# Linformer attention and a SwiGLU block on one core: VectorE's and GpSimd's side work at other tiles, half of the diagonal k' copies on ScalarE

## The chip, the cores and the metric

The kernel runs on one core of a Trainium2 chip. The metric is device microseconds of one execution; of a set of runs the median is given.

## The reference

Attention over 8 batches, 8 heads, 1024 tokens and head dimension 64, in which `E` and `F` first project the 1024 keys and values to 64 each, and then a SwiGLU block over the 8192 tokens with 512 model and 1536 inner dimensions. Inputs and output are float32.

```python
k_proj = np.einsum('ks,bhsd->bhkd', E, k)
v_proj = np.einsum('ks,bhsd->bhkd', F, v)
scores = 1.0 / np.sqrt(64) * np.matmul(q, k_proj.transpose(0, 1, 3, 2))
attn = softmax(scores)                      # the row maximum is subtracted first
x = np.matmul(attn, v_proj)                 # heads side by side: (8192, 512)
g = x @ w_gate
out = (g / (1 + exp(-g)) * (x @ w_val)) @ w_out
```

## The kernel before

**Tiles and slots.** The 8192 tokens are 16 chunks `c` of 512, two for each batch. The SwiGLU of a chunk takes 12 tiles `f`, one for each 128 of the 1536 inner columns; a loop written out by hand runs over all 192 tiles `t`. Each tile has two slots, 2t and 2t+1. In a tile come, in this order: the gate matmul (`f_g`, L536), what is put at slot 2t, the value matmul (`f_v`), the list `late[t]`, what is put at slot 2t+1. The order in which this Python issues work is the order of every engine's queue. `place(b)` puts the attention of batch b into the 24 tiles from slot s0 = 48(b-1) on. Those 24 tiles are called the turn of batch b below, and tiles and slots are counted from its start: tiles 0 to 11 are chunk 2b-2, tiles 12 to 23 are chunk 2b-1. Tiles 0 to 23 of the turn of batch 2 are tiles 24 to 47 of the whole.

**SwiGLU of a tile.** ScalarE takes silu of the gate from PSUM (`th`, L563; in some tiles as tanh with two VectorE steps, L560, L681, L684, since tanh needs no change of ScalarE's table beside exp), and VectorE multiplies it with the value product into `hT` (L678). From chunk 3 on the value products of pairs of tiles are made in seven smaller products instead of eight (`p_34`, `p_1`, `p_52`, `p_76`, matmuls at L616). They need sums of x (`p_x`, L607: m = 4, 3, 1 and 6 with 7 together) and sums of the weights (`p_w`, L595). Their results are put together by a ScalarE copy (L644), VectorE sums (L647, L627) and the product with silu (L634, which needs both tiles' silu, L646 and L556). L652 is ScalarE's copy of product 1.

**Down projection.** The 1536x512 product for chunk c-1 is made during chunk c, likewise in seven products m for each of two halves p (`f_m`, matmuls at L762, in the order m = 3, 4, 5, 2, 1, 6, 7). They need sums of `hT` (`h_sum`, L745): m = 5 and 2 by GpSimd in 12 small pieces a chunk, m = 1, 6 and 7 by VectorE in one piece each. After m = 4 ScalarE copies (L779) and GpSimd adds (L781); after m = 6 VectorE adds the m = 1 product out of PSUM (L791) and GpSimd subtracts (L792, after L791); the m = 7 product adds to the region that L791 reads, so it waits for L791; after it VectorE writes the output tile (L797, which needs L792), and SP sends it. For p = 0 the products 1 and 6 lie in tile 4 of the chunk and 7 in tile 5, for p = 1 in tiles 10 and 11.

**Attention of a batch.** `u_KV` projects k and v; ScalarE and VectorE copy the results (L195, L200). `u_KT` turns k' and writes it in four copies into the diagonal tile `BD` (L298, L299), from which the score matmuls read (`u_S`, L378). There are eight parts of the scores, each with an exponential on ScalarE into one of four buffers `ee` (L386), a row sum and reciprocal on VectorE (`u_R`, L408, L409), and the normalised product on GpSimd (`u_N`, L423, called N below, with a small running sum `zsum`, L439). Part 7 uses the buffer of part 3. SP turns q (`u_TD`, L355) and the probabilities (`u_AD`, L362) by DMA; `u_PVt` multiplies with v' (L482), and ScalarE copies to `xT` (L491). A ScalarE change between exp and silu is a table load. The loads of the next batch's k, v and q go through GpSimd's queue.

**The watch.** `u_sum` and `u_flag` add `zsum` up and make a flag out of it with a one-column matmul (L902, L903, L907); all engines read the flag near the end, and only if it is set does a second, general program run.

Of the kernel before, what the change touches and what calls it, by code (L numbers as in the profile page):

```python
# [26 lines left out]
NFT = DFF // P  # L27
# [4 lines left out]
HF = NFT // 2  # L32
# [11 lines left out]
def kernel(  # L44
# [19 lines left out]
    nc = tc.nc  # L64
# [98 lines left out]
    def bank(where, shape, dt, name):  # L163
        if where == "a" and ring["wide"]:
            where = "aaz"[ring["n"] % 3]
            ring["n"] += 1
        if where == "v":
            v_turn[0] ^= 1
        pool, tag = banks[where]
        if where in "vw":  # L170
            tag += str(v_turn[0] ^ (where == "w"))
        return pool.tile(shape, dt, name=name, tag=tag)

    def copy(eng, out, in_):
        (nc.scalar.copy if eng is nc.scalar else eng.tensor_copy)(out=out, in_=in_)
# [94 lines left out]
    def turn_ksp(t, b, g):  # L270
        nc.tensor.matmul(
            out=t[:, 2 * g : 2 * g + 2, :].rearrange("p a k -> p (a k)"),
            lhsT=ksp[b][:, 2 * g : 2 * g + 2, :].rearrange("p h d -> p (h d)"),
            rhs=ident_bf[:],
            start=True,
            stop=True,
        )

    def u_KT(b, at="a", prs=(0, NPAIR)):

        t = bank(at, [P, NPAIR, KP], FP32, "kTp")
        for pr in range(*prs) if b > 1 or maxed else ():
            nc.tensor.matmul(
                out=t[:, pr, :],
                lhsT=ks[b % 2][:, 2 * pr : 2 * pr + 2, :].rearrange("p h d -> p (h d)"),
                rhs=ident_bf[:, 0:KP],
                start=True,  # L290
                stop=True,
            )
        for g in range(2) if b < 2 and not maxed else ():
            turn_ksp(t, b, g)
        bd = BD[b % 2][:].rearrange("p (a c) k -> p a c k", c=2)
        for c in range(2):
            src = t[64 * c : 64 * c + 64, slice(*prs)]
            nc.vector.tensor_copy(out=bd[0:64, slice(*prs), c, 0:64], in_=src)  # L298
            nc.vector.tensor_copy(out=bd[64:128, slice(*prs), c, 64:128], in_=src)  # L299

    def u_KT0(prs, ats, engs):
# [558 lines left out]
    def put(s, fn, *a):  # L860
        slots[s].append((fn, a))

    def place(b):
        s0 = 48 * (b - 1)
        if b == 1:
            put(22, u_TD, 1, 0)
            put(29, u_K1, 1)
            put(32, u_KT, 1)
            put(40, u_V1, 1)
            sa = (35, 36, 37, 38, 41, 42, 43, 44)  # L870
            put(41, u_AD, 1, 0)
            put(30, u_TD, 1, 1)
            put(47, u_AD, 1, 1)
            put(46, u_PVt, 1, 0, (0, 1), ("aa", "av"))
        else:
            if b == 2:
                put(s0 + 10, u_KV, b)
            else:
                put(s0 + 8, u_KV, b, "kv", (0, H), "v")
            put(s0 + (13 if b == 2 else 11), u_KT, b)  # L880
            put(s0 + (9 if b == 2 else -6), u_TD, b, 0)
            put(s0 + (11 if b == 2 else -4), u_TD, b, 1)
            sa = [s0 + j for j in ((15, 15, 17, 17) if b == 2 else (13, 13, 15, 15)) + (25, 25, 27, 27)]
            put(s0 + 29, u_AD, b, 0)
            put(s0 + 42, u_AD, b, 1)
            put(s0 + 44, u_PVt, b, 0, (0, 1), ("aa", "yz"))
        for j in range(NJ):
            put(sa[j], u_S, b, j)
            at = sa[j] + 1 if b == 1 else s0 + (
                16, 17 + (b > 2), 20, 22, 31, 33, 36, 38)[j]  # L890
            put(at, u_R, b, j)
            put(at, u_N, b, j)
        put(s0 + (68 if b == 1 else 56), u_PVt, b, 1, (0, 1), ("aa", "yz"))
# [20 lines left out]
    def general():  # L914
# [6 lines left out]
        with tc.For_i(0, B) as turn, tc.manual_schedule():  # L921
            turn_of.append(turn)
            b = 0
            load_k(b)
            load_v(b)
            u_KV(b)
            u_KT(b)
            for ch in range(CH):
                c = CH * b + ch
                load_q(b, ch)  # L930
                for u in range(4 * ch, 4 * ch + 4):
                    u_T(b, u)
                    u_S(b, u)
                    u_R(b, u)
                    u_N(b, u)
                    u_A(b, u)
                u_PVt(b, ch, (0, 1), ("aa", "yz"))
                for f in range(NFT):
                    f_g(c, f)
                    f_v(c, f)  # L940
                for m in (1, 2, 5, 6, 7):
                    h_sum(c, m, 0, HF, nc.vector)
                for n in range(14):
                    f_m(c, n)

    with tc.manual_schedule():
# [3 lines left out]
        for i in range(2):  # L950
            nc.scalar.dma_start(
                out=kraw[i][:],
                in_=k[0, 2 * i : 2 * i + 2].rearrange("h (p j) d -> p h (j d)", j=NJ),
# [125 lines left out]
        for b in range(1, B):  # L1079
            place(b)  # L1080
        for b in range(2, B):
            s0 = 48 * (b - 1) - (20 if b == 3 else 24)
# [10 lines left out]
        late = defaultdict(list)  # L1093
# [4 lines left out]
        for c in range(1, NC):  # L1098
            for f in range(HF):
                for m in (5, 2):  # L1100
                    at = (8, 7, 11, 11, 10, 11)[f] if c > 2 else HF + f
                    late[c * NFT + at].append((h_sum, c, m, f, f + 1))
            if c == NC - 1:
                late[c * NFT + HF + 1].append((h_sum, c, 6, 0, HF, nc.vector))
                for f in (0, 2, 4):
                    for m in (1, 7):
                        late[c * NFT + HF + f + 1].append((h_sum, c, m, f, f + 2, nc.vector))
            else:
                for i, m in enumerate((1, 6, 7)):
                    late[(c + 1) * NFT + 1 + i].append((h_sum, c, m, 0, HF, nc.vector))  # L1110
                for n, f in enumerate((0, 1, 2, 3, 4, 4, 5, 6, 7, 8, 9, 10, 10, 11)):
                    late[(c + 1) * NFT + f].append((f_m, c, n))

        for p, ts in ((5, (26, 27, 28, 28, 28)), (8, (29, 29, 31, 31, 31)), (2, (42, 42, 43, 43, 43))):
            for m, t in zip((1, 2, 5, 6, 7), ts):
                late[t].append((p_w, m, p))
        for c in range(3, NC):
            for i, m in enumerate((4, 3, 1, 67)):
                if c == 3:
                    t = c * NFT + (2, 2, 3, 3)[i]  # L1120
                elif c % 2:
                    t = c * NFT - (7, 7, 3, 3)[i]
                else:
                    t = c * NFT + (-1, -1, 0, 0)[i]
                late[t].append((p_x, c, m))
        for p, cs in PAIRED.items():
            for c in cs:
                late[c * NFT + p].append((p_1, c, p))

        for s, fn in ((38, u_sum), (40, u_flag), (88, u_bad)):  # L1130
            put(48 * (B - 2) + s, fn)
        for t in range(NIT):
            c, f = divmod(t, NFT)
            ring["wide"] = c < 2
            i = 1 if t < 2 else None
# [42 lines left out]
```

## Time and profile before

| | |
|---|---|
| median of 3 runs | 564.73 us (564.32 to 565.6) |
| the profiled execution | 566.03 us |
| its span, first to last instruction | 564.5 us |
| mean granted TensorE clock | 0.997 |
| busy: PE, VectorE, GpSimd, ScalarE | 532.3, 429.3, 324.2, 289.6 us |

The profile is one execution. Its page gives busy times and the chain of work that ended last; further views give, for every engine, who waited for whom, and the instructions in order of time. In timeline rows the columns are start in us, duration in us, engine, line, operation, tiles, shapes and count; brackets hold the idle time of the engine before the instruction and what ended it. The ends of matmuls are modelled.

### The profile page before, as it was taken

How to read it: one execution, taken by the hardware profiler on the slowest of the kernel's cores; microseconds unless marked ns; L12 is line 12 of the kernel's file. 1: busy time of each engine (PE TensorE's matmuls, PEld its weight loads, DVE VectorE, ACT ScalarE, POOL GpSimd, SP SyncE). 2: the span in 40 equal slices, each digit the busy share in tenths (PEclk: the TensorE clock that was granted, in tenths of full speed). 3: DMA queues.
4: the chain of work that ended last, by engine and by line, in shares of the span. 5: the costliest groups of instructions: out<-in, count | busy, mean ns of one | idle time of the engine just before them, and what ended most of it. 6: DMA issues, size and time to landing. Idle time of an engine off the chain costs nothing.

```text
span 564.5 us, 9975 instructions
## 1 busy us (share of the span) xinstructions
PE 532.3 (94%) x3712; PEld 336.1 (60%) x3780; DVE 429.3 (76%) x724; ACT 289.6 (51%) x515; POOL 324.2 (57%) x428
## 2 busy tenths in 40 slices
PE   7999999998999999999999999999999997999996
PEld 4654445565566566566666566666666655566665
DVE  3787886759878788787887787877977878586664
ACT  3564363763456634646546464564455662453431
POOL 6861593555824967068661786437773465534344
PEclk9999999999999999999999999999999999899999
DMA  9999979749800598007961199213990121200113
GB/s 198 191 198 189 186 130 177 143 97 199 190 2 37 105 212 169 38 1 152 198 135 39 39 162 222 66 39 75 164 244 4 39 74 39 74 6 35 38 39 114
DMA packets 112228, 62.94 MB, mean 112 GB/s; under 512 B 65968, under 2 KB 103856, under 8 KB 112176
## 3 DMA queue, kind: packets, MB, share of 16 engines
q0 software_dynamic: 43952, 29.49, 36.5%
q1 hardware_dynamic: 67392, 31.46, 22.4%
q10 hardware_dynamic: 832, 1.31, 0.8%
q8 instruction: 30, 0.49, 0.4%
q14 instruction: 22, 0.18, 0.1%
HBM read 60.29 MB, written 16.78 MB: 137 GB/s over the span
## 4 chain that ended last, share of the span: by engine, by line
PE 74%; DVE 15%; issue 5%; POOL 3%; DMA 2%; ACT 2%; DVEq 0%; ACTq 0%; POOLq 0%
PE gps L536 22%; PE yps L762 19%; PE vps L536 16%; PE vps L616 8%; DMA wv<-in_moe_w_val_dram 2%; PE kvp L187 2%; PE sc L378 2%; DVE hs L745 2%; PE yps L696 2%; DVE sx L627 2%; DVE ts L647 1%; PE pv L482 1%; DVE hT L678 1%; DVE hT L634 1%; DVE zr L408 1%
## 5 line engine op out<-in xcount | busy, mean ns | idle before, releaser
L536 PE MATMUL gps<-xT,wg 128*128 128x512 bf16 (+1 forms) x727 | 193.0, 378 | 1.8
L745 POOL TENSOR_TENSOR hs<-hT 128x256 bf16<-128x256 bf16 x180 | 125.8, 729 | 5.7 <-DVE hT L678 4.9
L536 PE MATMUL vps<-xT,wv 128*128 128x512 bf16 (+1 forms) x459 | 118.9, 376 | 1.4 <-DMA wv<-in_moe_w_val_dram 0.8
L762 PEld LDWEIGHTS <-hs 128*128 128x128 bf16 x900 | 88.1, 98 | 34.0 <-issue 13.5
L536 PEld LDWEIGHTS <-wg 128*128 128x128 bf16 x776 | 74.3, 98 | 52.0 <-issue 1.1
L423 POOL TENSOR_TENSOR AAd<-ee,zr 128x512 bf16<-128x512 f32 x56 | 62.5, 1115 | 64.9 <-DVE zr L409 34.9
L563 ACT ACTIVATE th<-gps 128x512 f32<-128x512 f32 x82 | 49.0, 597 | 95.2 <-PE gps L536 86.9
L792 POOL TENSOR_TENSOR tt<-tt,ysb 128x512 f32<-128x512 f32 x28 | 35.6, 1273 | 95.9 <-DVE tt L791 95.9
L762 PE MATMUL yps<-ws,hs 128*128 128x256 bf16 x540 | 68.6, 272 | 10.6 <-DVE tt L791 10.5
L536 PEld LDWEIGHTS <-wv 128*128 128x128 bf16 x480 | 45.2, 98 | 50.9 <-issue 6.5
L678 DVE TENSOR_TENSOR hT<-th,vps 128x512 bf16<-128x512 f32 x82 | 55.4, 676 | 26.1 <-PE vps L536 22.0
L634 DVE TENSOR_TENSOR hT<-thp,sx 128x512 bf16<-128x512 f32 x74 | 56.8, 767 | 6.8 <-ACT thp L556 2.2
L781 POOL TENSOR_TENSOR tt<-xs 128x256 f32<-128x256 f32 x30 | 29.9, 997 | 55.1 <-ACT xs L779 55.1
L627 DVE TENSOR_TENSOR sx<-ts,vps 128x512 f32<-128x512 f32 x74 | 50.1, 677 | 15.0 <-PE vps L616 12.8
L762 PE MATMUL yps<-ws,hT 128*128 128x256 bf16 x360 | 48.8, 273 | 0.5
L762 PE MATMUL yps<-wo,hs 128*128 128x256 bf16 x360 | 49.0, 274 | 0.1
L745 DVE TENSOR_TENSOR hs<-hT 128x1536 bf16<-128x1536 bf16 (+1 forms) x49 | 48.2, 989 | 0.0
L644 ACT COPY sx<-vps 128x512 f32<-128x512 f32 x37 | 21.7, 586 | 51.4 <-PE vps L616 50.8
L408 DVE TENSOR_REDUCE zr<-ee 128x8 f32<-128x512 f32 x64 | 43.2, 674 | 4.9 <-ACT ee L386 4.9
L762 PEld LDWEIGHTS <-hT 128*128 128x128 bf16 x360 | 35.2, 98 | 13.2
L681 DVE SCALAR_TENSOR_TENSOR s<-th,gps 128x512 f32<-128x512 f32 x35 | 23.6, 673 | 21.6 <-ACT th L560 20.8
L647 DVE TENSOR_TENSOR ts<-sx 128x256 f32<-128x256 f32 x37 | 27.0, 729 | 16.7 <-ACT sx L644 16.2
(135 smaller groups left out, 741.6 us busy)
## 6 DMA issues: line engine op xcount, KB each, us to landing
out_dram<-ysb SPq DMA_DIRECT2D x27, 512.0 KB, 2.9
qb<-in_q_dram POOLq DMA_DIRECT2D x14, 512.0 KB, 16.9
kb<-in_k_dram POOLq DMA_DIRECT2D x7, 1024.0 KB, 8.9
vb<-in_v_dram POOLq DMA_DIRECT2D x7, 1024.0 KB, 13.9
wo<-in_moe_w_out_dram POOLq DMA_DIRECT2D x2, 768.0 KB, 21.6
out_dram<-ysb SPq DMA_DIRECT2D x6, 256.0 KB, 2.4
kraw<-in_k_dram ACTq DMA_DIRECT2D x2, 512.0 KB, 4.9
qb<-in_q_dram POOLq DMA_DIRECT2D x4, 256.0 KB, 8.0
```

Of the source, the lines that this page charges most:

```text
L408: nc.vector.reduce_sum(out=z, in_=e[:], axis=AX.X)
L423: eng.tensor_tensor(out=a.rearrange("p j h k -> p h j k"), in0=ee.pop((b, u))[:], in1=r.unsqueeze(3).to_broadcast([P, 4, 2, KP]), op=ALU.mult,
L536: nc.tensor.matmul(out=ps[:, ts], lhsT=(wg, wv)[w][:, kt, f * P : (f + 1) * P], rhs=x[:, kt, ts], start=(kt == 0), stop=(kt == NKT - 1),)
L563: nc.scalar.activation(out=th[:], in_=ps[:], func=AF.Silu)
L616: nc.tensor.matmul(out=ps, lhsT=w[:, kt], rhs=xs[:, kt], start=(start and kt == 0), stop=(kt == 1), skip_group_check=True,)
L627: nc.vector.tensor_tensor(out=out, in0=a.unsqueeze(1).to_broadcast([P, 2, HT]), in1=b, op=op)
L634: nc.vector.tensor_tensor(out=h, in0=th, in1=v, op=ALU.mult)
L647: nc.vector.tensor_tensor(out=ts[:, 0], in0=sx[:, 0], in1=sx[:, 1], op=ALU.add)
L678: nc.vector.tensor_tensor(out=hT[c][:, f, :], in0=th[:], in1=ps[:], op=ALU.mult)
L745: eng.tensor_tensor(out=hs[c, m][:, fs, :], in0=quarter(hT[c], *a)[:, fs], in1=quarter(hT[c], *b)[:, fs], op=op,)
L762: nc.tensor.matmul(out=ps, lhsT=lhsT, rhs=ws[m][:, f, :] if rhs is None else rhs, start=(start and f == 0), stop=(f == HF - 1), skip_group ...
L792: nc.gpsimd.tensor_tensor(out=t[:], in0=t[:], in1=yo[c, p][:, 1:3], op=ALU.subtract)
```

## The change

Five things move, and one changes engine. In `u_KT`, for batches from 2 on, the two copies into rows 0 to 63 of `BD` go to ScalarE. In `place`, the row sums and products of all eight parts go to later slots, and the second turn of the probabilities from slot 42 to 43, which is behind the first turn of the next batch's q on SP's queue. The VectorE sum for m = 7 goes from tile 3 of a chunk to tile 4, behind L791. The weight sums for p = 2 go from tiles 42 and 43 to 32 to 35, and one for p = 8 from tile 31 to 30. The sums of x for the odd chunks go from 7 and 3 tiles before the chunk (2 and 3 tiles into it for chunk 3) to its first tile; for even chunks they stay. The watch's sum and flag go from slots 38 and 40 of the last batch to 44 and 50.

```diff
@@ u_KT @@
         for c in range(2):
             src = t[64 * c : 64 * c + 64, slice(*prs)]
-            nc.vector.tensor_copy(out=bd[0:64, slice(*prs), c, 0:64], in_=src)
+            copy(nc.scalar if b > 1 else nc.vector, bd[0:64, slice(*prs), c, 0:64], src)
             nc.vector.tensor_copy(out=bd[64:128, slice(*prs), c, 64:128], in_=src)
@@ place @@
-            put(s0 + 42, u_AD, b, 1)
+            put(s0 + 43, u_AD, b, 1)
...
             at = sa[j] + 1 if b == 1 else s0 + (
-                16, 17 + (b > 2), 20, 22, 31, 33, 36, 38)[j]
+                17, 17 + 2 * (b == 2), 21 if b == 2 else 19, 23, 35, 37, 40, 41)[j]
             put(at, u_R, b, j)
             put(at, u_N, b, j)
@@ the list late @@
-                for i, m in enumerate((1, 6, 7)):
+                for i, m in enumerate((1, 6)):
                     late[(c + 1) * NFT + 1 + i].append((h_sum, c, m, 0, HF, nc.vector))
                 for n, f in enumerate((0, 1, 2, 3, 4, 4, 5, 6, 7, 8, 9, 10, 10, 11)):
+                    if n == 6:
+                        late[(c + 1) * NFT + 4].append((h_sum, c, 7, 0, HF, nc.vector))
                     late[(c + 1) * NFT + f].append((f_m, c, n))
...
-        for p, ts in ((5, (26, 27, 28, 28, 28)), (8, (29, 29, 31, 31, 31)), (2, (42, 42, 43, 43, 43))):
+        for p, ts in ((5, (26, 27, 28, 28, 28)), (8, (29, 29, 30, 31, 31)), (2, (32, 33, 33, 34, 35))):
...
             for i, m in enumerate((4, 3, 1, 67)):
-                if c == 3:
-                    t = c * NFT + (2, 2, 3, 3)[i]
-                elif c % 2:
-                    t = c * NFT - (7, 7, 3, 3)[i]
-                else:
-                    t = c * NFT + (-1, -1, 0, 0)[i]
+                t = c * NFT + (0 if c % 2 else (-1, -1, 0, 0)[i])
                 late[t].append((p_x, c, m))
...
-        for s, fn in ((38, u_sum), (40, u_flag), (88, u_bad)):
+        for s, fn in ((44, u_sum), (50, u_flag), (88, u_bad)):
             put(48 * (B - 2) + s, fn)
```

## Prediction

> **What bounds the kernel now.** The page first: which engine is busy and what the last chain is made of.
>
> ```profile
> PE 532.3 (94%) x3712; PEld 336.1 (60%) x3780; DVE 429.3 (76%) x724; ACT 289.6 (51%) x515; POOL 324.2 (57%) x428
> PE 74%; DVE 15%; issue 5%; POOL 3%; DMA 2%; ACT 2%; DVEq 0%; ACTq 0%; POOLq 0%
> ```
>
> PE sets the time; a gain must come out of its 32 us that are not busy. So next the waits of PE alone (waiter, releaser: total us, times, longest).
>
> ```profile
> PE yps L762 <- DVE tt L791: 10.5, 11, 1.0
> PE sc L378 <- DVE BD L299: 4.5, 10, 0.7
> PE vps L616 <- DVE sx L627: 2.4, 2, 2.1
> PE bad L907 <- DVE sane L903: 2.2, 1, 2.2
> ```
>
> All four are VectorE being late in its queue. The timeline shows behind what. The steady turn is 67.26 us (the wait at 237.54 in the chain returns at 304.80), and each of batches 3 to 7 holds three such stalls; I read the turn of batch 4.
>
> ```profile
> 235.89 0.41 DVE L607 TENSOR_TENSOR xsa<-xT 128x512 bf16<-128x512 bf16 x1
> 236.23 0.41 DVE L298 CAST BD<-kTp 64x256 bf16<-64x256 f32 x1
> 237.54 0.43 DVE L299 CAST BD<-kTp 64x256 bf16<-64x256 f32 x1
> 238.02 0.55 PE L378 MATMUL sc<-BD,qTd 128*128 128x128 bf16 x7 [0.68 <-DVE BD L299]
> ...
> 250.34 0.68 DVE L408 TENSOR_REDUCE zr<-ee 128x8 f32<-128x512 f32 x1
> 251.73 0.41 DVE L791 TENSOR_TENSOR tt<-tt,yps 128x256 f32<-128x256 f32 x1
> 252.20 0.81 PE L762 MATMUL yps<-ws,hs 128*128 128x256 bf16 x6 [1.04 <-DVE tt L791]
> 255.05 1.04 POOL L423 TENSOR_TENSOR AAd<-ee,zr 128x512 bf16<-128x512 f32 x1
> 256.23 3.80 POOL L745 TENSOR_TENSOR hs<-hT 128x256 bf16<-128x256 bf16 x6
> 258.91 1.13 ACT L386 ACTIVATE ee<-sc 128x512 f32<-128x512 f32 x2
> 263.99 0.95 DVE L745 TENSOR_TENSOR hs<-hT 128x1536 bf16<-128x1536 bf16 x1
> 264.86 0.68 DVE L408 TENSOR_REDUCE zr<-ee 128x8 f32<-128x512 f32 x1
> 268.03 0.41 DVE L791 TENSOR_TENSOR tt<-tt,yps 128x256 f32<-128x256 f32 x1
> ```
>
> (1) Tile 5: two x sums and four k' copies stand before the first scores. (2) Tile 10: a row sum stands before L791, for which the seventh product waits. (3) Tile 16: the m=7 sum and a row sum stand before L791. A gap counts from the modelled end of the matmul before, about 0.17 us late (six matmuls of 0.11 from 236.09 end at 236.75; the score matmul starts at 237.12 with a gap of 0.21). So the stalls cost PE 0.38 + 0.85 = 1.23, 1.20 and 1.09 us: 3.5 a turn, 17.6 over five turns. Before them, in chunk 3, PE loses 0.79, 2.24, 0.37 and 0.46 us (131 to 145 us), 3.9 in all. The flag's matmul loses 2.34 at 479.18, and more follows it, in the windows by stretch (PE, PEld, DVE, ACT, POOL, then granted clock, DMA share, GB/s):
>
> ```profile
> 479.00:481.00 2.00, 1.82 (x14) 1.46 (x15) 1.23 (x4) 1.05 (x2) 1.59 (x3) 0.77 0.75 171
> 481.00:484.00 3.00, 3.00 (x14) 1.61 (x13) 0.59 (x2) 1.00 (x3) 1.54 (x3) 0.59 0.27 61
> ```
>
> Right after that gap TensorE runs below full clock: (1-0.77)x2 + (1-0.59)x3 = 1.7 us lost. No other stretch of the steady part does so, not even after the 2.24 at 137.16.
>
> **The change, part by part.** No arithmetic is added. Twelve copies (L298, 0.42 us each, 5.0 us) leave VectorE and come to ScalarE. ScalarE's price for 64x256 is not shown; its copies of 64x128 take 0.26 and of 64x512 0.59, its 128x256 0.37, so I take 0.37 (0.26 to 0.59): 0.74 a turn.
>
> *Tile 5.* The x sums (0.33 + 0.33 of queue) and two copies (0.85) go from before the scores. In their place: the m=7 sum (0.95) now follows L791 of tile 4, and the m=7 product waits for it. L791 starts at 232.77, the sum runs 233.15 to 234.10, PE was ready at 233.79: a new stall of 0.36. GpSimd's L792 (1.27), which would start at 233.33, waits for the sum and ends at 235.3; L647 waits for L792 (ends 235.6), L797 follows to 236.2, the two copies end at 236.55 and 236.98. ScalarE's two copies run after L652, 235.70 to 236.45, so they are not last. PE is ready at 236.75 + 0.36 = 237.11 and runs through. The second score matmul starts at 237.15 instead of 238.02: 0.9 gained net. Exp's table load now waits for the scores; the exponentials end at 239.9 instead of 239.46, but th(7) is done at 240.5, when L681 can start on VectorE anyway (240.4): nothing.
>
> *Tile 10.* Row sums 0 and 1 now both stand behind L647 of tile 8, 0.83 each, row sum 2 before the second L627, and two x sums (1.88 at 247.21) are gone. From L647 at 243.0: L647 0.45, two row sums 1.65, L627 0.66, L634 0.8, row sum 0.85, L627 0.7, L634 1.3 (held by an N product, as the L634 of 1.02 at 137.21 was), L678 0.65, L791 0.4: 250.45. PE is ready at 251.00 - 0.9 = 250.1 to 250.2. So 0.25 is left of 1.20: gained so far 1.75.
>
> *Tiles 11 to 17.* Here the change pays back. Row sum 3 moves from slot 22 to 23, behind L797, and its product N (L423) on GpSimd behind eight h sums instead of two. The eight run from 251.8 (L792's end): 8 x 0.645 = 5.2. At the same time the four x sums now stand at tile 12, two x sums more than there is quiet room for: those beside GpSimd's sums take 0.89 where they take 0.42 alone, and each holds GpSimd for about 0.4. I take 1.6 for the four (0.9, what the eight sums at 284.56 to 290.64 took over 5.2, to 2.0). So N runs from 258.45 to 259.5, where it ended at 256.09. The exponential of part 7 writes the buffer which that N reads, so it starts at 259.55: it was 259.46. ScalarE has then given back all that PE had won: L644, table load, L646, L652, L556 end at 263.6 (263.26). L634 goes 263.6 to 264.25, then L627, L634, L678, L791 end at 266.65, the m=7 sum at 267.5. The product starts at 267.55; it was 268.49. Kept: 0.9 a turn. Each us that N is earlier or later moves this by one, with a ceiling of about 1.9 from L791 and the sum in a row; bounds -0.1 to 1.9.
>
> [...]
>
> *Tiles 17 to 23.* Row sums 4 to 7 go to slots 35, 37, 40, 41. Each is 0.83 before an L627, and PE's next use of that bank is ready 0.1 or more after; nothing taken, 0.3 a turn if that cover is gone. The second transpose of the probabilities (slot 43) now stands on SP behind the q transpose, which waits for q to land (issued at 263.22, 16.2 us): its own landing moves from 285.8 to about 289. PV takes it at 295.17 - 0.9, so 5 us cover it; beyond, each us is a us.
>
> *Chunk 3 (tiles 36 to 47).* Stall 2.24 is L647 held from 131.93 to 135.12 by a q load, L792 and an N in a row; now q goes ahead and N behind. Of 0.79 some 0.25 stays for the m=7 sum; of the last two some 0.4. Gained 3.2 (2.0 to 3.8). The five weight sums for p=2 (0.28 clear, at worst 1.4 each) go to tiles 32 to 35, where VectorE idles 0.5 to 1.8 us a tile: nothing.
>
> *The flag.* Its sum stands at tile 22, where the last N has ended at about 280.4 on the turn's scale, as the sum comes up; the matmul comes three tiles later: 2.3 gained (1.8 to 2.34), and the 1.7 of slow clock.
>
> [...]
>
> **Sum.** 5 x 0.9 + 3.2 + 2.3 + 1.7 = 11.7 from the profiled execution, 566.03 us (span 564.5 and 1.5 around it): 554.3. The median of the runs, 564.73, is 1.3 lower, about the slow clock, which I assume it did not have: 564.73 - 10.0 = 554.7. I say 554.5.
>
> **Rivals.** *VectorE and GpSimd share better*: N ends a us earlier, 1.9 a turn; 554.5 - 5.0 = 549.5. For it: GpSimd idles 2.85 us before its N at 251.40, and the new order fills that. *The gain is given back whole*: N a us later, 0 a turn; only chunk 3 and flag count, 564.7 - 5.5 = 559 to 559.7. For it: the walk leaves 0.1 us at tiles 8 to 10, where VectorE is never idle. *Slower*: N, behind h sums and x sums, holds the exponential of part 7. From 2.0 us later than I have it (261.5) a turn loses 1.1, and five turns eat the 5.5 of flag and chunk 3; at 2.7 later a turn loses 1.8: 564.7 - 5.5 + 9 = 568. Against it: that needs the x sums to cost GpSimd over 3.6. That the change does not do what it says is excluded by the order of its instructions.
>
> **How the numbers follow.** Forecast 0.5; better sharing 0.25; given back 0.16; slower 0.08; 0.01 for the rest. Range: -0.1 to 1.9 a turn with chunk 3 and flag from 3.8 to 6.1 gives 549.1 to 561.4; with the spread of the runs (564.32 to 565.6) I say 548.5 to 561.5. A measurement here tells 0.2%, 1.1 us, from no change: faster 0.90, same 0.03, slower 0.07.
>
> **What would show it.** Right: PE's waits for BD gone, those for L791 replaced by shorter ones for L745 before L762, none on L907, no clock below 1 near 480; N of tile 11 ends after its eight h sums, and L386 waits for POOL. Wrong: a turn over 67.3 or under 65 us, or PV L482 waiting for a DMA.

## The result, and the profile after

| | before | changed |
|---|---|---|
| median | 565.66 us (6 runs, 564.32 to 566.01) | 556.43 us (6 runs, 556.3 to 556.6) |
| the profiled execution | 566.03 us, span 564.5 | 556.3 us, span 554.7 |
| mean granted clock in it | 0.997 | 1.000 |

The ratio is 0.9842, with a 95% interval of 0.9829 to 0.9854: 9.2 us less, where 10 were forecast, and 1.9 us above the forecast of 554.5. Between the two profiled executions, from which the forecast's sum was made, the time fell by 9.7 us where 11.7 were written. First the line of busy times, then the waits of PE (waiter, releaser: total us, times, longest).

```profile
PE 532.3 (96%) x3712; PEld 334.4 (60%) x3780; DVE 436.0 (79%) x712; ACT 293.5 (53%) x527; POOL 343.9 (62%) x428
```

```profile
PE yps L762 <- DVE tt L791: 3.8, 5, 1.0
PE gps L536 <- ACT thp L646: 3.3, 5, 0.7
PE yps L762 <- DVE hs L745: 2.0, 13, 0.2
```

PE's work is the same, 532.3 us; VectorE and GpSimd are busier than before (429.3 and 324.2), although VectorE has twelve copies less, and yet the kernel is faster. The same instructions take longer where they lie beside the other engine's: the mean L634 is 0.86 us instead of 0.77, the mean L792 1.56 instead of 1.27. The waits for `BD` (L299), for L627 and at the flag are gone from the list. L791 still holds PE, 3.8 us instead of 10.5, and two waits are new: for the m=7 sum (L745), which was forecast, and of the gate matmul for ScalarE's silu (`thp`, L646), which was not.

Where the time came from follows when the start of each tile's gate weights is set against the same start before. Us gained at each place, for a turn the steady one of batches 4 to 7. A place is named here by the tile in which PE waits; the prediction and the expectations name some places by the tile before (10 for 11, 15 for 16, 16 for 17).

| place | forecast | measured |
|---|---|---|
| chunk 3, tiles 36 to 47 | 3.2 | 3.22 (0.46, 2.23, 0.31, 0.23) |
| turn, tiles 5 and 6 (m=7 sum, scores) | 0.9 | 0.58 (-0.33, +0.91) |
| turn, tile 11 (L791) | 0.85 | 0.30 |
| turn, tiles 15 to 17 | -0.85 | -0.25 (-0.18, -0.82, +0.75) |
| whole turn, with 0.06 at tile 21 | 0.9 | 0.70 (67.26 to 66.56); batch 3: 0.42 |
| flag and clock | 4.0 | 3.86 (2.83, 1.26, and -0.23 for the flag's matmul at its new place) |
| chunks 14 and 15 (m=7 sum) | 0 | -0.65 |

The timeline of the changed kernel, turn of batch 4 (start, duration, engine, line, operation; in brackets the idle time before and what ended it). Add 3.64, what had been gained before this turn, to come to the scale of the forecast.

```profile
230.48 0.83 PE L762 MATMUL yps<-ws,hs 128*128 128x256 bf16 x6 [0.15 <-DVE hs L745]
232.46 0.42 DVE L299 CAST BD<-kTp 64x256 bf16<-64x256 f32 x1
232.91 0.37 ACT L175 CAST BD<-kTp 64x256 bf16<-64x256 f32 x1 [0.72 <-DVE BD L299]
233.31 0.43 DVE L299 CAST BD<-kTp 64x256 bf16<-64x256 f32 x1 [0.43 <-ACT BD L175]
```

Here the m=7 product waits a little for its sum, and the k' copies, which were to run side by side, go in turn: ScalarE's second waits for VectorE's first, and VectorE's second for that. They end at 233.74, on the forecast's scale 237.38 where 236.98 was written.

```profile
234.57 0.69 DVE L634 TENSOR_TENSOR hT<-thp,sx 128x512 bf16<-128x512 f32 x1
...
241.36 1.04 POOL L423 TENSOR_TENSOR AAd<-ee,zr 128x512 bf16<-128x512 f32 x1
242.52 1.61 DVE L634 TENSOR_TENSOR hT<-thp,sx 128x512 bf16<-128x512 f32 x1
242.54 1.04 POOL L423 TENSOR_TENSOR AAd<-ee,zr 128x512 bf16<-128x512 f32 x1
...
247.68 0.82 PE L762 MATMUL yps<-ws,hs 128*128 128x256 bf16 x6 [0.71 <-DVE tt L791]
248.99 6.06 POOL L745 TENSOR_TENSOR hs<-hT 128x256 bf16<-128x256 bf16 x8
251.75 2.77 DVE L607 TENSOR_TENSOR xsa<-xT 128x512 bf16<-128x512 bf16 x3
255.01 1.04 POOL L423 TENSOR_TENSOR AAd<-ee,zr 128x512 bf16<-128x512 f32 x1
256.08 0.60 ACT L386 ACTIVATE ee<-sc 128x512 f32<-128x512 f32 x1 [1.06 <-POOL AAd L423]
259.12 1.02 PE L536 MATMUL gps<-xT,wg 128*128 128x512 bf16 x3 [0.66 <-ACT thp L646]
264.20 0.83 PE L762 MATMUL yps<-ws,hs 128*128 128x256 bf16 x6 [0.15 <-DVE hs L745]
```

The row sums of parts 0 and 1 now stand in one slot, so their products N follow each other on GpSimd, and the second falls beside L634. That L634 takes 1.61 us where the one at 234.57, with GpSimd idle, takes 0.69; so L791 is late and the m=7 product of tile 11 still waits 0.71. The row sums of parts 1 and 2 do not go to later slots, as the section on the change says of all eight: from batch 3 on they go one slot earlier, from 18 to 17 and from 20 to 19.

GpSimd then works through eight h sums, N of part 3 comes behind them, the exponential of part 7 waits 1.06 for it, and ScalarE is late with `thp` for the gate matmul of tile 16. The m=7 product of tile 17, which had waited 0.92 for L791, now waits 0.15 for its sum.

At the flag, the timeline and the windows that answer to those of before:

```profile
483.59 0.19 PE L907 MATMUL bad<-sane 128*1 128x1 f32 x2
```

```profile
479.00:481.00 2.00, 2.00 (x14) 1.22 (x13) 1.20 (x3) 0.53 (x1) 1.79 (x2) 1.00 1.05 238
481.00:484.00 3.00, 2.95 (x19) 1.53 (x18) 3.00 (x5) 0.90 (x2) 3.00 (x6) 1.00 0.45 175
```

The one-column matmul has no bracket, it waits for nothing, and the clock stays at 1.00 where it was 0.77 and 0.59.

### The profile page after: what moved, and what is told of

It is laid out like the page before. It is cut to its first block, busy times and chain, and to the rows that moved or that the text cites. A ratio compares the mean times of both kernels' runs of the same rounds, so it can differ in the third digit from the quotient of the medians.

```text
span 554.7 us, 9971 instructions
## 1 busy us (share of the span) xinstructions
PE 532.3 (96%) x3712; PEld 334.4 (60%) x3780; DVE 436.0 (79%) x712; ACT 293.5 (53%) x527; POOL 343.9 (62%) x428
## 5 line engine op out<-in xcount | busy, mean ns | idle before, releaser
L745 POOL TENSOR_TENSOR hs<-hT 128x256 bf16<-128x256 bf16 x180 | 133.7, 773 | 7.0 <-DVE hT L678 4.4
L792 POOL TENSOR_TENSOR tt<-tt,ysb 128x512 f32<-128x512 f32 x28 | 43.7, 1560 | 101.0 <-DVE tt L791 98.9
L762 PEld LDWEIGHTS <-hs 128*128 128x128 bf16 x900 | 86.9, 98 | 31.6 <-issue 5.8
L563 ACT ACTIVATE th<-gps 128x512 f32<-128x512 f32 x82 | 49.0, 597 | 92.0 <-PE gps L536 87.2
L678 DVE TENSOR_TENSOR hT<-th,vps 128x512 bf16<-128x512 f32 x82 | 55.7, 679 | 23.0 <-PE vps L536 18.9
L634 DVE TENSOR_TENSOR hT<-thp,sx 128x512 bf16<-128x512 f32 x74 | 63.3, 856 | 6.4 <-ACT thp L556 1.8
L627 DVE TENSOR_TENSOR sx<-ts,vps 128x512 f32<-128x512 f32 x74 | 49.4, 667 | 12.2 <-PE vps L616 10.9
L781 POOL TENSOR_TENSOR tt<-xs 128x256 f32<-128x256 f32 x30 | 27.1, 905 | 46.5 <-ACT xs L779 46.5
L745 DVE TENSOR_TENSOR hs<-hT 128x1536 bf16<-128x1536 bf16 (+1 forms) x49 | 47.9, 985 | 0.0
L386 ACT ACTIVATE ee<-sc 128x512 f32<-128x512 f32 x64 | 36.2, 602 | 9.6 <-POOL AAd L423 5.3
L647 DVE TENSOR_TENSOR ts<-sx 128x256 f32<-128x256 f32 x37 | 25.4, 688 | 16.8 <-ACT sx L644 16.8
```

The costliest lines, as they stand in the source:

```text
L386: nc.scalar.activation(out=e[:].rearrange("p h j k -> p (h j k)"), in_=ps[:].rearrange("p a k -> p (a k)"), func=AF.Exp, scale=scale,)
L563: nc.scalar.activation(out=th[:], in_=ps[:], func=AF.Silu)
L627: nc.vector.tensor_tensor(out=out, in0=a.unsqueeze(1).to_broadcast([P, 2, HT]), in1=b, op=op)
L634: nc.vector.tensor_tensor(out=h, in0=th, in1=v, op=ALU.mult)
L678: nc.vector.tensor_tensor(out=hT[c][:, f, :], in0=th[:], in1=ps[:], op=ALU.mult)
L745: eng.tensor_tensor(out=hs[c, m][:, fs, :], in0=quarter(hT[c], *a)[:, fs], in1=quarter(hT[c], *b)[:, fs], op=op,)
```

## The experiments

Each kernel was run beside the kernel before, whose median was 565.4 to 566.1 us on these chips. "Span" is that of the profiled execution, to be set against 554.7 for the changed kernel.

### The flag alone

The kernel before with one line of the change.

```diff
-        for s, fn in ((38, u_sum), (40, u_flag), (88, u_bad)):
+        for s, fn in ((44, u_sum), (50, u_flag), (88, u_bad)):
```

> The kernel before with the watch's sum and flag alone moved to slots 44 and 50. Theory: the wait of L907 (2.17 us, 2.34 on PE) goes, and with it the stretch at half clock that follows it (3.413 us at half clock is 1.7 us of work): 3.6 to 4.1 us less than the profile of before (span about 560.6), with the clock at 1.00 throughout; against the median of before somewhat less, if not all of its runs have the slow stretch. [...]

Measured: 562.17 us, ratio 0.9945 (0.9928 to 0.9961), span 560.6, which is 3.9 less than the 564.5 before; the medians differ by 3.2. More than the 2.3 of the stall came back, so in these two profiled executions the slow clock belongs to the stall. In the clock row of its page (40 slices, in tenths of full speed) every slice is at 9, where the page of before has an 8 in the slice from 479.8 to 493.9 us. The mean clock is 0.998 in it; of its four runs one, of 563.13 us, has 0.997, the others 0.998 to 1.000.

### Part 3 one slot earlier

```diff
-                17, 17 + 2 * (b == 2), 21 if b == 2 else 19, 23, 35, 37, 40, 41)[j]
+                17, 17 + 2 * (b == 2), 21 if b == 2 else 19, 23 if b == 2 else 22, 35, 37, 40, 41)[j]
```

> The changed kernel with row sum and product of part 3 back at slot 22 for batches 3 to 7. In the changed kernel gps waits 0.66 us (0.83 on PE) in tile 15 for silu L646, because the exponential of part 7 waited 1.06 us for the product of part 3, which stands behind eight h sums on GpSimd. Theory: that wait of L386 for POOL goes, the wait of gps L536 for L646 goes, the turn falls from 66.56 to 65.7 us, 4 us in five turns (span about 550.7); the row sum now stands before L678 and L797 of tile 11, for which nobody on PE waits. Rival (the table load and the exponentials keep ScalarE late by themselves): gps still waits 0.5 us or more and the span stays within 1 us of 554.7.

Measured: 553.01 us, ratio 0.9776 (0.976 to 0.9793), span 551.4. The exponential's wait for GpSimd and the gate matmul's wait for ScalarE are both gone, and a turn gains 0.69. So the new wait of tile 16 does come from N of part 3.

### The sums of x at their old tiles

```diff
-                t = c * NFT + (0 if c % 2 else (-1, -1, 0, 0)[i])
+                if c == 3:
+                    t = c * NFT + (2, 2, 3, 3)[i]
+                elif c % 2:
+                    t = c * NFT - (7, 7, 3, 3)[i]
+                else:
+                    t = c * NFT + (-1, -1, 0, 0)[i]
```

> The changed kernel with the sums of x for odd chunks where they were before (7 and 3 tiles ahead of the chunk, 2 and 3 tiles into it for chunk 3). Theory: two sums before the scores of tile 5 cost 0.7 us there, two more in tile 9 make L791 of tile 10 1.0 to 1.9 us later, while the h sums of GpSimd in tiles 10 and 11 run 0.9 us faster, so that the exponential of part 7 no longer waits 1.06: a turn of 66.9 to 67.6 us, span 556.5 to 560. Rival (GpSimd's delay by the sums in tile 12 is what costs most): gps no longer waits in tile 15 and the span is the same or lower than 554.7.

Measured: 561.03 us, ratio 0.9929 (0.9908 to 0.9949), span 559.1. Three of its waits of PE:

```profile
PE yps L762 <- DVE tt L791: 5.7, 5, 1.4
PE sc L378 <- DVE BD L299: 3.2, 5, 0.6
PE vps L536 <- DVE sx L627: 2.1, 5, 0.4
```

The scores wait for BD again, and L791 and L627 are later; the wait for `thp` is gone. A turn loses 0.67 at tile 6 and 0.96 at tile 11, and gets 0.67 back at tiles 15 and 16, since without the x sums beside it GpSimd has N in time: its list has no wait of the exponential for N, where that of the changed kernel has five, 5.3 us in all. The move of the x sums is worth 4.4 us net.

### All four copies on VectorE

```diff
-            copy(nc.scalar if b > 1 else nc.vector, bd[0:64, slice(*prs), c, 0:64], src)
+            copy(nc.vector, bd[0:64, slice(*prs), c, 0:64], src)
```

> The changed kernel with all four k' copies on VectorE again. In the changed kernel the four copies run one after another although they are on two engines (0.37, 0.42, 0.37, 0.43 in turn, each waiting for the one before), so ScalarE's share saves only what VectorE would else run after L797. Theory: four copies from 232.46 take 4 x 0.43 and end at 234.2 instead of 233.74: 0.4 to 0.5 us a turn, 2.0 to 2.5 us in five turns (span about 557). Rival (the copies on ScalarE bring nothing, since they alternate): within 0.5 us of 554.7. Second rival (VectorE's 0.85 counts whole): 4.3 us, span 559.

Measured: 557.97 us, ratio 0.9865 (0.9849 to 0.9882), span 556.4. It costs 0.35 a turn at the scores and nothing elsewhere:

```profile
PE sc L378 <- DVE BD L299: 2.5, 5, 0.5
```

That is 1.7 us for the one edit that changes an engine, where 2.0 to 2.5 were expected. It is little because the copies on two engines run in turn (the waits of 0.72 and 0.43 in the timeline of the changed kernel).

### ScalarE's two copies ahead of VectorE's

```diff
-        for c in range(2):
-            src = t[64 * c : 64 * c + 64, slice(*prs)]
-            copy(nc.scalar if b > 1 else nc.vector, bd[0:64, slice(*prs), c, 0:64], src)
-            nc.vector.tensor_copy(out=bd[64:128, slice(*prs), c, 64:128], in_=src)
+        for r in range(2):
+            for c in range(2):
+                rows = slice(64 * r, 64 * r + 64)
+                copy(nc.vector if r or b < 2 else nc.scalar, bd[rows, slice(*prs), c, rows], t[64 * c : 64 * c + 64, slice(*prs)])
```

> The changed kernel with ScalarE's two k' copies issued first and VectorE's two after them, instead of in turn. Theory: the copies run one after another because each engine waits for the other's last copy out of the same PSUM tile; ordered in pairs there is one such wait instead of three. ScalarE's pair ends near 232.6 (it starts at 231.83), VectorE's pair runs 232.6 to 233.45 instead of to 233.74, the second score matmul is not held (0.31 us on PE now): 0.3 us a turn, 1.5 us in five turns, span about 553.2. Rival (the second pair starts later than now, and the first score matmul needs one copy of each pair): the first score matmul waits 0.2 us or more instead of the second, and the span is within 0.5 us of 554.7.

Measured: 555.4 us, ratio 0.9814 (0.9791 to 0.9837). The profiled execution lost 1.3 us in the first 62 us, before any copy that differs; from there each turn is 0.23 shorter (that of batch 4 by 0.81, of which 0.54 come at tile 11), and the second score matmul no longer stands idle.

```profile
233.69 0.88 DVE L175 CAST BD<-kTp 64x256 bf16<-64x256 f32 x2 [0.18 <-ACT BD L175]
```

VectorE's two copies now wait once, 0.18. The order of the copies costs 0.23 a turn in the changed kernel; the medians differ by 1.0.

### The m=7 sum early in even chunks and in the last

```diff
-                for i, m in enumerate((1, 6)):
+                early = (c + 1) % 2 == 0 or c == NC - 2
+                for i, m in enumerate((1, 6, 7) if early else (1, 6)):
...
-                    if n == 6:
+                    if n == 6 and not early:
```

> The changed kernel with the sum for m=7 at tile 3 again in even chunks and in the last chunk, and behind L791 of tile 4 in the other odd ones alone. Theory: in the even chunks the m=7 product had not waited before, and now waits 0.15 us by the gap, about 0.3 on PE, in each of chunks 4, 6, 8, 10, 12, 14 and in chunk 15: 7 x 0.3 = 2.1 us come back, and L792, now 1.85 us because the sum holds it, falls to 1.27 there; span about 552.6. Rival (the stall is only moved, since L792 and L647 decide when the copies of k' start): chunks 14 and 15 alone gain, 0.6 us, span about 554.1.

Measured: 553.78 us, ratio 0.9788 (0.9765 to 0.9811), span 552.3. Against the changed kernel it gains 0.43 a turn, 0.33 of it at tile 5, and 0.33 in each of chunks 14 and 15. In the even chunks the change's move of this sum is a plain loss, for which nothing later gives anything back.

### Part 3 earlier and part 2 later

```diff
-                17, 17 + 2 * (b == 2), 21 if b == 2 else 19, 23, 35, 37, 40, 41)[j]
+                17, 17 + 2 * (b == 2), 21, 23 if b == 2 else 22, 35, 37, 40, 41)[j]
```

From batch 3 on part 3 goes from slot 23 to 22 and part 2 from 19 to 21.

> The kernel of x2 (part 3 at slot 22) with part 2 at slot 21, behind L791 of tile 10, instead of 19. Theory: L791 of tile 10 is late (gap 0.71, 0.88 on PE, in five turns) because three row sums (0.83 each) and two L634 held by N products stand between L647 of tile 8 and it; without row sum 2 it comes 0.85 to 1.4 earlier, and the stall goes: 4.4 us less than x2 (span 551.4), about 547.0, if the products of parts 2 and 3, now behind two h sums, still end before the exponentials of parts 6 and 7 need their buffers. Rival (they do not): L386 waits for POOL again and gps for L646 in tile 15, and the span is 550 to 551.5.

Measured: 555.56 us, ratio 0.9815 (0.979 to 0.9839), span 554.3. Tile 11 gains 0.87 a turn, but tile 14 loses 1.53, by a wait that neither theory named. From its waits and its timeline:

```profile
PE yps L762 <- POOL hs L745: 7.3, 5, 1.8
```

```profile
252.65 5.14 POOL L745 TENSOR_TENSOR hs<-hT 128x256 bf16<-128x256 bf16 x6
257.04 0.28 PE L762 MATMUL yps<-wo,hs 128*128 128x256 bf16 x1 [1.38 <-POOL hs L745]
```

Two N products now stand ahead of six h sums on GpSimd, and the products of the down projection that read these h sums come a tile or two later. Both theories followed the products N to the exponentials that wait for them, and not to the h sums behind them on GpSimd.

### All row sums at their old slots

```diff
-            put(s0 + 43, u_AD, b, 1)
+            put(s0 + 42, u_AD, b, 1)
...
-                17, 17 + 2 * (b == 2), 21 if b == 2 else 19, 23, 35, 37, 40, 41)[j]
+                16, 17 + (b > 2), 20, 22, 31, 33, 36, 38)[j]
```

> The changed kernel with all row sums and products at the slots of before (and the turn of the probabilities at 42). Theory: without two x sums between, L791 of tile 10 is 1.9 us earlier than before but has a row sum in front of it: stall 0.2 to 0.9; the product of part 3 is early, so gps does not wait in tile 15 (0.8 a turn better); but row sum 4 stands before L791 of tile 16 and the m=7 sum behind it: 0.3 to 0.9 a turn worse. Together within 1.5 us of 554.7, so that the moves of the row sums as a whole bring little once x sums and the m=7 sum have moved. Rival (the moves of the row sums are what brings most): 558 or more.

Measured: 553.65 us, ratio 0.9782 (0.9758 to 0.9806), span 552.3: 2.4 us faster than the changed kernel, where at most 1.5 were expected, with its largest edit undone. A turn gains 0.87 at tile 11 and 0.67 at tiles 15 and 16, and loses 0.94 in tile 17:

```profile
259.00 0.68 DVE L408 TENSOR_REDUCE zr<-ee 128x8 f32<-128x512 f32 x1
...
263.51 0.83 PE L762 MATMUL yps<-ws,hs 128*128 128x256 bf16 x6 [1.10 <-DVE hs L745]
```

Row sum 4 stands before L627, L634, L678 and L791 here, and so before the m=7 sum, which starts only at 262.50. So the eight moved row sums are two groups of opposite sign: parts 0 to 3 seem better at the old slots, parts 4 to 7 at the new; the next run tries it.

### Only parts 0 to 3 at their old slots

```diff
-                17, 17 + 2 * (b == 2), 21 if b == 2 else 19, 23, 35, 37, 40, 41)[j]
+                *((17, 19, 21, 23) if b == 2 else (16, 18, 20, 22)), 35, 37, 40, 41)[j]
```

> The changed kernel, with the row sums and products of parts 0 to 3 at their old slots 16, 18, 20 and 22 in the turns of batches 3 to 7; parts 4 to 7 and the second turn of the probabilities stay at their new slots. Theory: the run with all the old slots gained 1.6 us a turn at tiles 10 and 15, where parts 0 to 3 hold L634 and part 7's exponential, and lost 0.9 a turn in tile 17, where parts 4 and 5 stand before the m=7 sum. The two halves lie apart, so with only the first put back the gain stays whole: 5 x 1.6 = 8.0 less than the changed kernel, a span of 546.7 and a median of about 548; no wait of L386 for POOL over 0.5 us, no wait of the gate matmul L536 for ScalarE, and the m=7 product of tile 17 waits no more than 0.3. Rival: the row sums of parts 4 and 5 only took place of another wait there, and the down projection of tiles 16 and 17 is late on VectorE in any order once PE comes 1.6 earlier: the two halves do not add, 0.7 or less a turn, a span of 551 or more.

Measured: 548.24 us, ratio 0.9697 (0.9682 to 0.9711), span 547.0. The two halves do add up: 7.7 us less than the changed kernel, 1.6 a turn. Its largest waits of PE:

```profile
PE yps L762 <- DVE hs L745: 2.1, 13, 0.2
PE warm L985 <- DVE zeros L963: 1.4, 1, 1.4
```

The waits for L791 and for `thp` are gone, and in the steady part, apart from one wait of 0.3, only the 0.2 of the m=7 sum is left.

### The three repairs together

The kernel of the last experiment, with the edits of the copies in pairs and of the m=7 sum early.

> The kernel with parts 0 to 3 at the old slots, and with it the m=7 sum at tile 3 in even chunks and in the last, and ScalarE's two k' copies ahead of VectorE's two. Theory: the three repairs lie at different tiles (10 and 15; 5; 6) and add up: 8.0 + 2.9 (as the run with the m=7 sum early measured) + 1.1 (five turns of 0.23) = 12 less than the changed kernel, a span of 542 to 543.5, median about 544.5. Rival: what PE wins at tiles 5 and 6 it waits for at tile 10, where VectorE is never idle and L791 would then be last: only the 0.8 of the last chunks is added to the first repair, a span of about 546.

Measured: 545.31 us, ratio 0.9642 (0.9628 to 0.9655), span 543.7: 3.3 under the one repair and 11.0 under the changed kernel, the best of all. That is just outside the 542 to 543.5 expected: a turn gains 0.33 at tile 5 and 0.14 at tile 6 on top, less than the two repairs gained apart (0.43 and 0.23), and chunks 14 and 15 another 0.6. Between 215 and 300 us no gap of PE is over 0.16 us. In the turn it is now PE that sets the time.

### The flag soon behind the last part

```diff
-        for s, fn in ((44, u_sum), (50, u_flag), (88, u_bad)):
+        for s, fn in ((41, u_sum), (43, u_flag), (88, u_bad)):
```

> The changed kernel, with the watch's sum and flag at slots 41 and 43 of the last batch, as close behind the last part as they were before the change (36, 38, 40 there; 41, 41, 43 here). Theory: PE stands at the flag's matmul until VectorE has the sum, which needs the last N's zsum: a gap of 2 to 2.8 us. Whether the clock falls after it depends on how much of it lies within one 3.41 us window of the clock's records: with more than about two thirds of the window idle it falls to 0.5 for the next window (another 1.3 to 1.7 us), so 2.3 more than the changed kernel without the fall, 4.0 with it: a median of 558.7 or 560.4. Rival: the fall of the clock has nothing to do with the gap and belongs to the place in the program; then the changed kernel, at full clock there, would have been spared it by chance, and this one shows clock 1.0 with any gap, or 0.5 with a gap well under 2 us.

Measured: 560.37 us, ratio 0.9906 (0.989 to 0.9922). The profiled execution, span 560.4, in its timeline and windows (busy us of PE, PEld, DVE, ACT, POOL, then granted clock, DMA share, GB/s):

```profile
477.51 0.19 PE L907 MATMUL bad<-sane 128*1 128x1 f32 x2 [3.31 <-DVE sane L903]
```

```profile
475.00:477.00 2.00, 0.00 (x0) 0.00 (x0) 0.00 (x0) 0.00 (x0) 2.00 (x4) 1.00 0.00 0
477.00:479.00 2.00, 1.49 (x6) 0.65 (x7) 1.67 (x5) 0.00 (x0) 0.07 (x1) 0.67 0.54 123
479.00:481.00 2.00, 2.00 (x14) 0.65 (x12) 0.62 (x1) 0.60 (x1) 0.00 (x0) 0.50 0.62 139
```

The stall is 3.3 us, above the 2 to 2.8 expected, since N of part 7 now has two more h sums ahead of it. The clock falls again, to 0.67 and 0.50 in the two stretches from 477 to 481. Of the six runs three show a mean clock of 0.996 to 0.997 and take 561.1 to 562.0, and three show 0.999 and take 559.5 to 559.6. The rival, that the place in the program does it, falls: in the changed kernel PE does not stall there, and none of its six runs has a mean clock below 0.998. But the stall is not enough either: by the mean clocks, the same program loses the 1.7 in some executions and keeps it in others.

### The weight sums at their old tiles

```diff
-        for p, ts in ((5, (26, 27, 28, 28, 28)), (8, (29, 29, 30, 31, 31)), (2, (32, 33, 33, 34, 35))):
+        for p, ts in ((5, (26, 27, 28, 28, 28)), (8, (29, 29, 31, 31, 31)), (2, (42, 42, 43, 43, 43))):
```

> The changed kernel, with the weight sums back at their old tiles (p = 2 at 42 and 43, one of p = 8 at 31). Theory: of the 3.2 us that chunk 3 gained, the 2.23 at 137 and the 0.41 at 132 come of the row sums, products and transposes, and only the last two, 0.31 and 0.23 (at 141.4 and 144.7 before, where three weight sums of 1.75 in all stand before L678's reader and L647), come of the weight sums: 0.5 slower than the changed kernel, a span of 555.3 and a median of 556.9, with two short waits of L616 for VectorE in tiles 43 and 44. Rival one, as the forecast has it: they cost nothing at either place, 556.4. Rival two: they stood behind the 2.24 stall as well, and 2 us or more come back, 558.5.

Measured: 558.25 us, ratio 0.9872 (0.985 to 0.9894), span 556.5, 1.8 more than the changed kernel. It loses 0.43 and 1.14 at the two places that the theory named, which is more than its 0.5: with the row sums at their new slots, two of them (140.47 and 141.59) join the three weight sums in front of L647 and L627.

```profile
138.81 1.74 DVE L595 TENSOR_TENSOR wp<-wv 128x256 bf16<-128x256 bf16 x3
143.11 0.60 PE L616 MATMUL vps<-xsa,wo 128*128 128x256 bf16 x4 [1.19 <-DVE sx L627]
```

## Why the prediction was right, step by step

**What bounds it.** VectorE being late in its queue was the cause at all the stalls; the best version has the same arithmetic and ends 20 us sooner than the kernel before, by order and by twelve copies on another engine.

**Chunk 3 and the flag.** 3.2 was written and 3.22 came. For the flag 2.3 and 1.7 were written, 4.0 in all, and 3.86 came; the border between its parts of 2.83 and 1.26 lies inside the slow stretch, so only the sum can be compared. In the profiles with the flag alone and with the flag soon the slow clock goes with the stall: no slice of the clock row below 9 in the one, 0.67 and 0.50 from 477 to 481 us in the other. That the median of 564.73 was without the slow clock was assumed; all six runs together have a median of 565.66.

**Tiles 5 and 6.** 0.58 instead of 0.9. The m=7 sum was sized well (0.33 for 0.36). So was ScalarE's copy, 0.37; its price for 64x256 was in the profile of before, at L195, although the prediction says it is not shown. What failed is the step "ScalarE's two copies run after L652, ... so they are not last": they were counted as if they ran beside VectorE's. They take turns, and the run with the copies in pairs puts 0.23 on it.

The wait of 0.43 is between copies of the same rows. The 0.72 is not: there ScalarE's copy reads rows 64 to 127 of the PSUM tile and waits for VectorE's of rows 0 to 63. All four copies read one PSUM tile and write one `BD`; which of the two makes them take turns was not tried.

**Tile 10.** "L634 0.8" was the mis-sized term: 1.61, where the one at 234.57 takes 0.69. N of part 1 starts 0.02 after it and lasts 1.04. With this L791 ends at 247.62, on the forecast's scale 251.26 instead of 250.45, and 0.30 is gained there instead of 0.85 (by the prediction's own figures, 0.25 left of 1.20, it would be 0.95). In the turn of batch 3 the second L634 takes 1.44 instead of 1.15, and nothing is gained there. The forecast counted a hold by N at the second L634, from the 1.02 at 137.21, and not at the first.

**Tiles 11 to 17.** The mechanism held: N behind eight h sums, the exponential behind N, ScalarE late after it. On the forecast's scale N starts at 258.65 (258.45 was written, though its terms 251.8 + 5.2 + 1.6 make 258.6), the exponential at 259.72 (259.55) and the m=7 product at 267.84 (267.55). Two errors cancel in this, by luck. GpSimd began its eight h sums 0.83 later than written, for L791's sake, and the four x sums cost it 0.98 instead of 1.6: three h sums took 0.85 beside an x sum and one 1.11, where they take 0.67 alone. That is about a quarter of a us for each x sum, where the forecast took 0.4, and no run shows the 2.0 that it set as the upper end. The place was wrong: PE gives the time back at tile 16, where the gate matmul waits 0.66 for `thp`, and not at the m=7 product of tile 17. This moved no time, since whatever is lost at the one is not waited for at the other.

**Tiles 17 to 23, the second turn of the probabilities, the weight sums.** Costed at nothing at their new places; the waits of PE show none of them. What the old places would have cost shows in the runs: 0.94 a turn for parts 4 and 5 once tiles 11 and 16 are clear, and 1.6 to 1.8 us for the weight sums.

**Chunks 14 and 15.** Left out of the sum: the m=7 product waits for its sum there too, and nothing pays for it, 0.65 us in all. The turns brought 3.2 (4 x 0.70 and 0.42) instead of 4.5, and the flag 0.14 less than written. These three, 1.3, 0.65 and 0.14, account for the 1.9 between forecast and result.

**The rivals.** "Better sharing" needed N a us earlier and did not come; the run with part 3 a slot earlier shows that 0.7 a turn was there to be had. "Given back whole" named the right mechanism, but the turn kept 0.70. The slower case needed N at 261.5, and it was at 259.69 by its end.

**What stays open.** Why the clock falls in some executions and not in others after the same stall. In the profile before the granted clock is at 0.50 from 480.07 to 483.48 us, 3.413 us by its record; ahead of that it is at 1.00 for 474.45 us, which is 139.0 times as long, and behind it for 81.92 us, 24.0 times. In the changed kernel it is at 1.00 for 549.55 us, 161.0 times. In windows of 3.413 us, counted back and on from the fall, PE's idle time filled 69% of the window ahead of the fall in the profile before (64% by the rows alone, without the 0.17 us of the modelled ends), and 94% in the kernel with the flag soon. The 2.24 us stall at 137.16 filled 54% of its window, and the idle time from 558.57 to 561.99 us 57%, both by the rows, and no fall followed either. So it is an estimate, from these four windows, that what goes with the fall is how much of a stall lies in one window, and not its length alone. Shifting a stall within such a window was not tried.

## What to carry to other kernels

Walk a moved step through every queue that it stands in: a row sum brings its product on GpSimd, and that product delays h sums behind it and the VectorE instruction beside it; here 1.6 us a turn hung on four such steps. Measure the parts of a bundle apart: two of these moves (row sums 0 to 3, the m=7 sum in even chunks) lost time, while row sums 4 to 7, the sums of x, the copies, the weight sums and the flag gained, and with the two undone and the copies reordered 11 us more came off. The m=7 sum in odd chunks and the second turn of the probabilities were not measured alone. Where a stall goes, price what is next on all engines, not on the engine that was late.

## What the runs showed of the hardware

In the profile before, PE stood 2.17 us by the row at the flag's matmul (479.18), 2.34 with the modelled ends, and the granted clock was then 0.50 from 480.07 to 483.48 us, for one window of 3.413 us, half of which, 1.7 us, is lost. In the profile with the flag soon the stall was 3.31 us by the row, and the clock was 0.67 from 477 to 479 us and 0.50 from 479 to 481. In the changed kernel, with no stall there, it was 1.00 from 479 to 484. The fall did not come in every execution of a program: of eleven runs of the kernel before on one chip, nine show a mean clock of 0.995 to 0.997 and take 565.3 to 566.3 us, and two show 1.000 and take 564.4; with the flag soon, three of six show 0.999 and take 559.5 to 559.6.

On ScalarE in the profile before, each of the 25 table loads at a change between exp and silu (L386, L646, L563) took 1.28 us, and none stands at the tanh of L560.
